# Fewer, longer copies of the sums of v, and a first dense slice converted before the experts begin

## Chip, core and metric

The kernel runs on one core of a Trainium2 chip. The metric is the device time of one execution in microseconds (us), as the median of repeated runs. Engines: PE (TensorE, matmuls and transposes), DVE (VectorE), ACT (ScalarE), POOL (GpSimd), SP (SyncE, which here only sends DMAs).

## What is computed

Three stages on 1536 tokens (2 batches of 768) of width 512 (8 heads of 64):

```python
k_sum = k.reshape(B, H, nb, 32, D).max(axis=3)         # blocks of 32
v_sum = v.reshape(B, H, nb, 32, D).mean(axis=3)
scores = concat([where(|i - j| < 16, q @ k.T / 8, -1e9), q @ k_sum.T / 8 + log(32)])
x = softmax(scores) @ concat([v, v_sum])               # attention, per head
# mixture of experts: tokens with x @ w_skip > 0 go to one of 8 experts (D=512, F=1024)
e = argmax(x @ w_gate); x = x + gate * (relu(x @ w1[e]) @ w2[e])
# dense stage: 512 -> 2048 -> 512
h = x @ w_in; g = where(h >= 1, h, where(h <= -1, 0, (h + 1)**2 / 4)); out = g @ w_out
```

## The kernel before

**Attention** (function `attention`) works on 24 units, twelve per batch. The order of every step is written out by hand as a list of words in `FIRST`; each word is one step, its numbers are its arguments, and each engine executes its own steps in the order of the list. K and k turn q and k (PE transposes, copies by DVE and ACT), S is a unit pair's scores, n and e the maximum and the exponential, T and t turn the probabilities, V multiplies them with v, d, f and x divide. q and lv are loads of q, k and v on SP's queue.

v lies in twelve tiles per batch (`vtile`), three to a buffer of `tails`; rows 0 to 95 of a tile are a window of v, rows 96 to 119 the 24 block sums of v. The sums are made per batch b and half of the heads c: v (three groups of matmuls), u (DVE copies them into `sums`), w (a matmul folds them into PSUM), z (ACT copies the folded sums to `sums`), and then twelve times y (`vgive`, line 361), each copying 24 x 256 sums into one tile. `DIRECT` (line 27) says how many of the twelve are copied directly from PSUM, alternately by ACT and DVE; the others are copied by POOL from `sums`. V of a tile needs its y.

**Routing** is woven into the same list: R, r, L, l compute the gate's scores of one tile of 128 tokens, ga and ia are generators (`r3`, `r4`) of small DVE steps, P is a prefix sum on PE, and sc scatters the finished tiles, by POOL's indirect DMA, into sorted lists in DRAM (`xf`). Tiles go in the groups 0-2, 3-5, 6, 7-8, 9-10, 11. E counts the tokens after tiles 0 to 6; from that ea, ec, ej choose the expert whose tokens form the first block, and `first` gathers it from DRAM. The tokens of a tile stand in one of nine buffers x0 to x8 (`xring`, line 258 for x7 and x8; `XTILE` says which tile uses which); tiles 9 and 10 are in x7 and x8. FX, FA, FB, FD compute the first block (128 tokens of one expert) on PE; FY adds it on DVE and scatters it. lo, ll, lr, le compute the rows of the other blocks; G0 to G3 and GL gather them, once tile 11 has been scattered. lF loads expert weights (1 MB each), W loads a slice of the dense weights (`ff_fetch`).

**Experts and dense stage** (function `experts`) follow the list `ORDER`. Per block p: X, x (transpose and copy), A, a (first matmul, ReLU), T, t, B (second matmul), y (add and scatter); U, P, Q, O are the second part of the largest block. R, r, l transpose the first 512 rows for the dense stage and split them into a high and a low part. Dense slices f = 0 to 15: the weights come as 64-bit numbers, and `bits` (line 1066) makes 32-bit floats of them in three DVE steps (words i, j, k), `high` (H, ACT) and `low` (L, DVE) split them into the two parts in `ffw`. M is the first dense matmul of a slice (12 matmuls of 512 columns), c, S, g, G its activation, N the second (12 matmuls). F fetches expert weights into buffers that earlier blocks free. `st["late"]` names the PSUM buffers in which the blocks' transposes go; M sets it to "h" from the first M on, since N0 takes the "tp" buffers for its results. After the list (`dense.rest`) the remaining slices run in a fixed loop; the dense stage has three chunks of 512 tokens.

Of the kernel before, what the change touches and what calls it, by code (L numbers as in the profile page):

```python
# [43 lines left out]
T7 j8 c5 M6 L7 k8 t7 N3 c6 S5 i9 j9 B7 g5 S6 H8 G5 N4 y7 M7 g6 L8 G6 k9 N5 c7 i10 j10 H9 S7 k10 g7 G7 N6 L9 i11
j11
# [5 lines left out]
K0.2.0 y0.0.1 T1 k0.2.0 q1.0.1 y0.0.0 S4 y0.0.2 z0.0 V0 t1 y0.0.3 y0.0.4 q1.1.1 n4 K0.2.1 e3 y0.0.5 K0.2.2 d0 y0.0.6
k0.2.1 V1 y0.0.7 k0.2.2 K0.2.3 h0.2 y0.0.8 m0.2 T2 y0.0.9 K0.3.0 t2 k0.2.3 y0.0.10 e4 T3 k0.3.0 b0.2 q1.2.0 K0.3.1
y0.0.11 f0 d1 K0.3.2 x0 q1.2.1 k0.3.1 V2 t3 k0.3.2 K0.3.3 h0.3 T4 m0.3 lv1.0.2 v0.1.0 t4 k0.3.3 b0.3 v0.1.1 f1 n5 S6
q1.3.0 x1 e5 d2 V3 f2 n6 v0.1.2 x2 q1.3.1 e6 T5 u0.1 V4 d3 n7 w0.1 K1.0.0 t5 f3 d4 x3 lv1.0.0 S8 y0.1.0 k1.0.0 z0.1
e7 f4 y0.1.2 y0.1.1 V5 x4 y0.1.3 T6 lv1.0.1 n8 y0.1.4 K1.0.1 t6 K1.1.0 d5 y0.1.5 k1.0.1 e8 T7 y0.1.6 k1.1.0 K1.0.2
# [10 lines left out]
S20 ga6 f15 t17 ga6 x15 e19 ga6 d16 P6 f16 E T18 n20 V17 ia6 t18 ea R7 ia6 ea ia6 e20 T19 ec ia6 ea ia6 ec sc6 ea ec
ea x16 r7 S22 ea n21 t19 ea d17 L7 e21 ea f17 ea x17 T20 ea R8 ej ea ej ea V18 ej rege l7 r8 ej n22 V19 t20 d18 n23
e22 T21 lF1.0 f18 lF1.1 d19 first x18 lF1.2 f19 L8 t21 lF1.3 x19 e23 l8 V20 ga7 ga7 R9 ga7 d20 ga7 T22 f20 ga7 x20 p7
V21 r9 ga7 ga7 ga7 P7 t22 d21 L9 f21 ia7 x21 T23 ia7 V22 l9 t23 ia7 R10 ia7 d22 FX ia7 f22 r10 sc7 x22 V23 Fx L10
lF2.0 d23 FA0.0 f23 l10 lF2.1 x23 ga9 R11 ga9 p9 ga9 FA0.1 ga9 r11 ga9 ga9 ga9 L11 ga9 P9 l11 FA0.2 ga11 ia9 ga11 ia9  # L70
# [1299 lines left out]
```

## Time and profile before

| | |
|---|---|
| runs, median (lowest to highest) | 466.08 us (464.23 to 466.92) |
| profiled execution | 467.6 us, span 465.9 us, mean granted clock 0.977 |
| PE busy | 441.9 us (95% of the span) |
| DVE, ACT, POOL busy | 264.8, 208.5, 75.7 us |
| DMA | 73.36 MB, mean 157 GB/s |

How to read it: the page divides the span into 40 slices and gives the busy share of each engine in each; the granted clock is the share of full speed (2.4 GHz) that TensorE got. PE's busy time counts slow matmuls as busy, so a stretch at half clock looks full. The attention takes about the first 93 us, the first block goes to 119 us, experts and dense slices are mixed to about 225 us, and the rest is the dense stage.

### The profile page before, as it was taken

To read this page: it belongs to the slowest core of one execution; us is meant where nothing else is said; L and a number is where in the kernel's file an instruction comes from. 1 tells how busy PE (TensorE), PEld (TensorE's weight loads), DVE (VectorE), ACT (ScalarE), POOL (GpSimd) and SP (SyncE) were. 2 spreads that over 40 slices of the span, in tenths; PEclk is the share of its full clock that TensorE was granted. 3 is DMA by queue.
4 is the path that set the end of the run, shared out by engine and by line. 5 is a ranking of instruction groups with operands and counts; after the bars stand their busy time and mean duration, and the time that the engine had idled before them with its cause. 6 is when DMAs were issued, how large, how long until landed. Compare 5 with 4: busy or idle time off the path is not lost.

```text
span 465.9 us, 8194 instructions
## 1 busy us (share of the span) xinstructions
PE 441.9 (95%) x3100; PEld 319.5 (69%) x3100; DVE 264.8 (57%) x625; ACT 208.5 (45%) x416; POOL 75.7 (16%) x171
## 2 busy tenths in 40 slices
PE   8989999869699999999999999999999999999993
PEld 4657767744345544557888787888888888888872
DVE  5567778925634884888989734333334444334341
ACT  4646668612343233547377764333333343333341
POOL 7314243412610311010100003000000030000003
PEclk9998999979889999999999999999999999999998
DMA  9989729899965999996367001000000020000002
GB/s 181 210 158 217 163 75 380 324 381 393 358 205 214 367 389 389 394 367 203 123 222 271 2 25 69 23 0 1 0 1 1 1 90 1 1 0 1 0 0 97
DMA packets 75008, 73.36 MB, mean 157 GB/s; under 512 B 48926, under 2 KB 57118, under 8 KB 74960
## 3 DMA queue, kind: packets, MB, share of 16 engines
q1 hardware_dynamic: 72144, 64.55, 44.8%
q0 software_dynamic: 2816, 8.20, 4.7%
q8 instruction: 26, 0.43, 0.4%
q14 instruction: 22, 0.18, 0.1%
HBM read 65.66 MB, written 7.70 MB: 157 GB/s over the span
## 4 chain that ended last, share of the span: by engine, by line
issue 50%; PE 17%; DMA 4%; POOL 2%; DVE 1%; SPq 1%; POOLq 0%; ACT 0%; ACTq 0%
PE hf L1134 5%; PE yp L963 4%; PE hp L941 3%; DMA w<-in_moe_w_dram 2%; POOL out_dram L1187 2%; PE yp L1003 1%; DMA x<-xf,re 1%; PE o L1175 1%; PE o L1176 1%; PE o L1177 1%; DVE x L968 1%; PE tph L951 0%; SPq L169 0%; PE tpx L929 0%; POOLq L1166 0%
## 5 line engine op out<-in xcount | busy, mean ns | idle before, releaser
L1134 PE MATMUL hf<-xh,ffw 128*128 128x512 f32 x384 | 127.0, 392 | 0.0
L1134 PEld LDWEIGHTS hf<-xh,ffw 128*128 128x128 f32 x384 | 72.1, 188 | 16.9 <-issue 1.9
L1175 PE MATMUL o<-ffw,g 128*128 128x512 f32 x192 | 76.5, 398 | 0.7 <-ACT g L1158 0.7
L1176 PE MATMUL o<-ffw,g 128*128 128x512 f32 x192 | 75.5, 393 | 0.0
L1177 PE MATMUL o<-ffw,g 128*128 128x512 f32 x192 | 74.9, 390 | 0.0
L1134 PE MATMUL hf<-xl,ffw 128*128 128x512 f32 x192 | 74.9, 390 | 0.0
L1153 DVE TENSOR_TENSOR hf<-hf,c 128x512 f32<-128x512 f32 x48 | 33.5, 698 | 60.0 <-ACT c L1144 43.7
L1143 ACT ACTIVATE hf<-hf,scal 128x512 f32<-128x512 f32 x32 | 21.2, 662 | 85.1 <-DVE c L1142 85.1
L1187 POOL DMA_INDIRECT out_dram<-ob,perm x12 | 11.7, 975 | 223.9 <-DVE ob L1186 160.6
L1162 DVE TENSOR_TENSOR g<-hf,g 128x512 fp32r<-128x512 f32 x48 | 33.1, 690 | 24.9 <-ACT g L1158 24.8
L1142 DVE TENSOR_SCALAR c<-hf 128x512 f32<-128x512 f32 x32 | 22.1, 691 | 37.5 <-PE hf L1134 37.5
L1158 ACT CAST g<-hf 128x512 fp32r<-128x512 f32 x48 | 28.1, 585 | 33.8 <-DVE hf L1153 31.5
L1175 PEld LDWEIGHTS o<-ffw,g 128*128 128x128 f32 x192 | 36.0, 188 | 10.0 <-issue 1.3
L1177 PEld LDWEIGHTS o<-ffw,g 128*128 128x128 f32 x192 | 36.0, 188 | 8.5 <-DVE g L1162 0.4
L1134 PEld LDWEIGHTS hf<-xl,ffw 128*128 128x128 f32 x192 | 36.1, 188 | 8.0 <-DVE xl L1124 0.4
L1176 PEld LDWEIGHTS o<-ffw,g 128*128 128x128 f32 x192 | 36.1, 188 | 6.9
L968 DVE SCALAR_TENSOR_TENSOR x<-yp,x 32x512 f32<-32x512 f32 (+1 forms) x28 | 20.8, 745 | 15.4 <-PE yp L963 14.7
L445 ACT ACTIVATE p<-s,nm 128x120 f32<-128x120 f32 x96 | 26.8, 371 | 5.1 <-DVE nm L439 5.0
L187 POOL DMA_INDIRECT xf<-x,ids x10 | 11.9, 1191 | 81.8 <-DVE ids L213 81.4
L1146 ACT ACTIVATE c<-hf,scal 128x512 f32<-128x512 f32 x16 | 11.0, 689 | 30.7 <-PE hf L1134 30.7
L1144 ACT ACTIVATE c<-c,scal 128x512 f32<-128x512 f32 x32 | 22.8, 712 | 0.0
L941 PE MATMUL hp<-w,xT 128*32 128x256 f32 (+1 forms) x224 | 21.6, 439 | 0.5 <-ACT xT L933 0.5
(224 smaller groups left out, 630.6 us busy)
## 6 DMA issues: line engine op xcount, KB each, us to landing
w<-in_moe_w_dram SPq DMA_DIRECT2D x32, 1024.0 KB, 12.4
raw<-in_moe_w_in_dram SPq DMA_DIRECT2D x16, 512.0 KB, 5.2
raw<-in_moe_w_out_dram SPq DMA_DIRECT2D x16, 512.0 KB, 6.0
pb<-in_v_dram SPq DMA_DIRECT2D x40, 96.0 KB, 3.6
raw<-in_k_dram SPq DMA_DIRECT2D x16, 192.0 KB, 4.4
raw<-in_q_dram SPq DMA_DIRECT2D x16, 192.0 KB, 4.4
x<-xf SPq DMA_DIRECT2D x8, 264.0 KB, 5.5
rows<-xf SPq DMA_DIRECT2D x1, 1024.0 KB
```

What stands on the lines that cost most here:

```text
L445: nc.scalar.activation(out=p[:, u], in_=s[:, u], func=AF.Exp, bias=nm[:, u:u + 1], scale=1.0)
L941: nc.tensor.matmul(hp[a], xT[:, kk], wx[p, 0][:, kk, m * f:m * f + m], start=kk == 0, stop=kk == 3)
L968: nc.vector.scalar_tensor_tensor(out=xg[0:n, 0:512], in0=yp[a], scalar=xg[0:n, 512:513], in1=xg[0:n, 0:512], op0=ALU.mult, op1=ALU.add)
L1134: nc.tensor.matmul(hp, w[:, 128 * kk:128 * kk + 128], a[:, kk], start=(n == 0), stop=(n == 11))
L1142: nc.vector.tensor_scalar(out=c, in0=hp, scalar1=-1.0, scalar2=1.0, op0=ALU.max, op1=ALU.min)
L1144: nc.scalar.activation(out=c, in_=c, func=AF.Square, bias=half, scale=0.5)
L1153: nc.vector.tensor_tensor(out=hp, in0=hp, in1=c, op=ALU.add)
L1158: nc.scalar.copy(out=g[:, 0], in_=hp)
L1162: nc.vector.tensor_tensor(out=o, in0=hp, in1=h.bitcast(F32), op=ALU.subtract)
L1175: nc.tensor.matmul(ops[ch][t], gh[:, a], hi, start=(f == 0), stop=False)
L1176: nc.tensor.matmul(ops[ch][t], gh[:, a], lo, start=False, stop=False)
L1177: nc.tensor.matmul(ops[ch][t], gl[:, a], hi, start=False, stop=(f == NF - 1))
```

## The change

The y words now copy three tiles at once (48 become 16), with the sums repeated by a broadcast; `GIVERS` names the engine of each. The buffers x7 and x8 become one tile, `x78`, whose first 1024 columns hold the bits of dense slice 0. The words i0, j0, k0, W1, H0, L0 go from the beginning of `ORDER` to the end of `FIRST`, as ci, cj, ck, W1, cH, cL. The switch of `st["late"]` goes from M to N. z1.1 is no longer there, as no copy of that half is made by POOL. Both lists are new for all engines: in `ORDER` M0 stands ahead of X0, and A1 ahead of A0.

```diff
-DIRECT = (4, 2), (2, 4)
+GIVERS = (("APPD", "PDPP"), ("ADPP", "ADAD"))
-        xring.extend(per.tile([128, XW], F32, name=f"x{i}") for i in (7, 8))
+        two_x = per.tile([128, 2, XW], F32, name="x78")
+        xring.extend(two_x[:, i] for i in range(2))
+        st["cv0"] = two_x.rearrange("p n c -> p (n c)")[:, 0:1024].rearrange("p (n c) -> p n c", n=2).bitcast(I32)
-        def vgive(b, c, j):
-            to = vtile(b, j)[96:120, 4 * c:4 * c + 4, 0:64]
-            if j >= DIRECT[b][c]:
-                nc.gpsimd.tensor_copy(out=to, in_=sums[c][96:120].rearrange("p (h d) -> p h d", h=4))
-            else:
-                (nc.vector.tensor_copy if j % 2 else nc.scalar.copy)(out=to, in_=st["vo", b, c][96:120])
+        def vgive(b, c, m):
+            to = tails[4 * b + m][96:120, :, 4 * c:4 * c + 4, 0:64]
+            by = GIVERS[b][c][m]
+            x = sums[c][96:120].rearrange("p (h d) -> p h d", h=4) if by == "P" else st["vo", b, c][96:120]
+            {"P": nc.gpsimd.tensor_copy, "D": nc.vector.tensor_copy, "A": nc.scalar.copy}[by](
+                out=to, in_=x.unsqueeze(1).to_broadcast([24, 3, 4, 64]))
 FIRST, before:
-V16 ga6 ia3 ga6 sc3 d15 p6 S20 ga6 f15 t17 ga6 x15 e19 ga6 d16 P6 f16 E T18 n20 V17 ia6 t18 ea R7 ia6 ...
-d22 FX ia7 f22 r10 sc7 x22 V23 Fx L10 lF2.0 d23 FA0.0 f23 l10 lF2.1 x23 ga9 R11 ga9 p9 ...
-FD0.0 Fb1 FD0.1 FD0.2 FD0.3 FD1.0 G0 FD1.1 FD1.2 G1 FD1.3 G2 FY G3 GL
 FIRST, after:
+V16 r7 ga6 S20 ia3 ga6 sc3 t17 d16 ga6 f16 ga6 p6 x16 T18 e19 ga6 n20 L7 V17 ga6 l7 ga6 n21 P6 t18 E e20 ia6 ...
+d22 ia7 FX ia7 f22 ia7 R10 x22 sc7 Fx l9 V23 r10 FA0.0 lF2.0 d23 f23 x23 lF2.1 L10 FA0.1 l10 ga9 ga9 R11 ...
+FD0.0 Fb1 lr ia11 lr sc11 lr lr FD0.1 FD0.2 FD0.3 ci FD1.0 cj FD1.1 ck FD1.2 W1 cH FD1.3 G0 cL G1 FY G2 G3 GL
 ORDER, before:
-Z0 R0 R1 r0 i0 R2 r1 l0 r2 l1 R3 l2 r3 X0 j0 x0 A0 l3 k0 W1 H0 L0 X1 F32 a0 F33 x1 T0 M0 t0 B0 i1 c0 j1 k1 H1 S0
-A1 y0 g0 X2 a1 G0 x2 L1 T1 A2 t1 M1 F50 a2 F40 F41 W2 F51 W4 X3 c1 B1 T2 y1 N0 ...
 ORDER, after:
+Z0 R0 R1 r0 R2 r1 r2 l0 l1 R3 l2 r3 l3 M0 X0 c0 X1 i1 j1 x1 x0 A1 S0 k1 g0 A0 F40 a1 G0 H1 L1 T1 F32 a0 X2 F33
+t1 T0 x2 B1 t0 B0 y1 M1 y0 E6 A2 c1 N0 F50 W2 F41 a2 S1 W3 F51 F42 X3 ...
         def M(f):
-            st["late"] = "h"
             bag["M", f] = dense.mm1(0, f)
+        def N(f):
+            st["late"] = "h"
+            dense.mm2(0, f)
```

## Rows read from the trace of the kernel before

**Rows 1.** PE's timeline: start us, us, engine, line, operation [idle before, releaser].

```profile
33.72 0.62 PE L348 MATMUL vs<-pb,picks 96*32 96x256 f32 x2 [1.26 <-DMA pb<-in_v_dram]
...
90.68 0.64 PE L504 MATMUL lp<-wg,xs 128*64 128x9 f32 x16
...
92.45 0.66 PE L493 MATMUL tpx<-ident,x 128*128 128x128 f32 x4
97.25 1.09 PE L225 MATMUL tpx<-ident,x 128*128 128x128 f32 x4 [4.14 <-DMA x<-xf,r]
```

**Rows 2.** POOL's timeline, same columns, 77 to 108 us.

```profile
77.77 4.21 POOL L364 COPY pb<-sums 24x256 f32<-24x256 f32 x12 [8.20 <-DMA xf<-x,si]
82.25 0.98 POOL L187 DMA_INDIRECT xf<-x,si  x1 [0.28 <-POOL pb L364]
...
86.10 0.98 POOL L187 DMA_INDIRECT xf<-x,si  x1 [0.30 <-DVE be L707]
90.19 1.06 POOL L182 DMA_INDIRECT x<-xf,r  x1 [3.12 <-DVE ohb L546]
...
107.98 0.98 POOL L187 DMA_INDIRECT xf<-x,si  x1 [0.30 <-DVE cnt L646]
```

**Rows 3.** DVE's timeline: tiles 3 to 5, tile 6, and FY.

```profile
76.91 0.29 DVE L596 CAST x<-meta 128x2 int32<-128x2 f32 x3
...
82.05 0.15 DVE L596 CAST x<-meta 128x2 int32<-128x2 f32 x1
...
118.62 0.75 DVE L822 SCALAR_TENSOR_TENSOR x<-yp,x 128x512 f32<-128x512 f32 x1 [6.25 <-PE yp L818]
```

**Rows 4.** The instructions of line 585: duration ns min/median/max, first and last start.

```profile
L585 DVE SCALAR_TENSOR_TENSOR sf<-meta,comp x6: 150/152/422, 64.0 to 109.6; 128x3 f32<-128x3 f32 x2, 128x1 f32<-128x1 f32 x2, 128x2 f32<-128x2 f32 x2
```

**Rows 5.** PE's timeline, 119 to 182 us: R0-R2, A0, A1, B4, A6.

```profile
119.43 1.53 PE L225 MATMUL tps<-ident,rows 128*128 128x128 f32 x12 [0.85 <-DVE x L822]
...
125.23 6.30 PE L941 MATMUL hp<-w,xT 128*64 128x512 f32 x16 [0.51 <-ACT xT L933]
...
139.16 1.93 PE L941 MATMUL hp<-w,xT 128*32 128x256 f32 x32
...
175.28 1.91 PE L963 MATMUL yp<-w,hT 128*32 128x512 f32 x12 [0.51 <-DMA w<-in_moe_w_dram]
...
178.72 3.65 PE L941 MATMUL hp<-w,xT 128*64 128x512 f32 x16
```

**Rows 6.** Windows: length, busy us (x) by engine, granted clock, DMA share, GB/s.

```profile
35.00:40.00 5.00, 5.00 (x75) 3.33 (x74) 3.21 (x10) 2.30 (x7) 1.79 (x5) 0.66 1.20 230
...
125.00:130.00 5.00, 4.77 (x12) 1.49 (x14) 2.77 (x4) 1.22 (x2) 3.09 (x3) 0.50 0.68 256
```

**Rows 7.** The chain that ended last, in order of time: start us, us, what.

```profile
111.23 0.97 DMA xf<-x,si
...
117.99 5.94 DMA x<-xf,re
...
132.88 2.77 PE hf L1134 x12
```

**Rows 8.** Groups by shape: line engine op, out<-in, xcount | busy us, mean ns.

```profile
L1077 DVE SCALAR_TENSOR_TENSOR cv<-raw,cv 128x1024 int32<-128x1024 int32 x16 | 19.6, 1223 | 0.5
...
L1091 ACT CAST ffw<-cv 128x1024 fp32r<-128x1024 f32 x16 | 16.6, 1039 | 7.2 <-DVE cv L1080 7.2
...
L364 POOL COPY pb<-sums 24x256 f32<-24x256 f32 x36 | 12.8, 399 | 30.9 <-ACT sums L359 22.5 <-DMA xf<-x,si 8.2
...
L1074 DVE TENSOR_SCALAR cv<-raw 128x1024 int32<-128x1024 int32 x16 | 11.0, 688 | 5.1 <-DMA raw<-in_moe_w_out_dram 5.0
...
L366 DVE COPY pb<-vso 24x256 f32<-24x256 f32 x6 | 2.6, 430 | 1.9 <-ACT sums L359 1.5 <-PE vso L356 0.2 <-ACT pb L366 0.2
...
L366 ACT COPY pb<-vso 24x256 f32<-24x256 f32 x6 | 2.1, 366 | 3.3 <-PE vso L356 2.8 <-DVE pb L366 0.5
```

More of the change, by code (lines that the diff above doesn't have):

```diff
@@ L44 @@
[L44 to L45 removed]
+Z0 R0 R1 r0 R2 r1 r2 l0 l1 R3 l2 r3 l3 M0 X0 c0 X1 i1 j1 x1 x0 A1 S0 k1 g0 A0 F40 a1 G0 H1 L1 T1 F32 a0 X2 F33
+t1 T0 x2 B1 t0 B0 y1 M1 y0 E6 A2 c1 N0 F50 W2 F41 a2 S1 W3 F51 F42 X3 g1 x3 G1 A3 T2 F60 a3 X4 t2 T3 x4 B2 t3 i2
+j2 N1 y2 A4 k2 B3 a4 W4 H2 E7 F43 F61 L2 F52 U0 F53 T4 u0 y3 X5 t4 P0 x5 i3 A5 j3 p0 k3 P1 a5 W6 H3 F62 L3 T5 i4
+p1 B4 t5 j4 k4 Q0 X6 q0 W5 y4 Q1 F63 x6 H4 F70 A6 q1 L4 M2 a6 i6 O0 c2 j6 k6 W7 H6 S2 g2 L6 G2 T6 i5 X7 o0 M3 x7
@@ L51 @@
[L51 to L55, printed above, removed]
@@ L66 @@
[L66 to L70, printed above, removed]
@@ L71 @@
-p11 ga11 FA0.3 ia9 ga11 ia9 ga11 ia9 FA1.0 Fa0 ga11 rows sc9 ga11 N P11 lF2.2 FA1.1 lo ia11 lF2.3 lo le lo lF3.0 le
-FA1.2 lo le lo le lF3.1 lo ia11 lo FA1.3 ia11 ll lr ll lr ll lr regl ia11 FB0 Fa1 lr ia11 lr sc11 lr FB1 Fb0 lr lr
-FD0.0 Fb1 FD0.1 FD0.2 FD0.3 FD1.0 G0 FD1.1 FD1.2 G1 FD1.3 G2 FY G3 GL
+q0.0.0 q0.0.1 q0.1.0 q0.1.1 Z7 K0.0.0 K0.0.1 lv0.0.0 k0.0.0 k0.0.1 h0.0 m0.0 Z3 K0.0.2 K0.0.3 k0.0.2 lv0.0.1 b0.0
+k0.0.3 Z3 K0.1.0 K0.1.1 k0.1.0 lv0.0.2 k0.1.1 h0.1 m0.1 Z3 K0.1.2 K0.1.3 k0.1.2 b0.1 q0.3.0 k0.1.3 S0 q0.2.0 v0.0.0
@@ new lines @@
+n0 n1 e0 q0.2.1 Z3 v0.0.1 S2 e1 q0.3.1 v0.0.2 lv0.1.1 n2 T0 u0.0 t0 n3 w0.0 e2 K0.3.0 lv0.1.0 T1 k0.3.0 y0.0.0 S4
+z0.0 misc V0 t1 y0.0.3 y0.0.1 e3 T2 d0 n4 y0.0.2 K0.2.0 K0.2.1 f0 lv0.1.2 k0.2.0 V1 t2 k0.2.1 K0.2.2 e4 x0 K0.2.3
+k0.2.2 T3 q1.0.0 k0.2.3 V2 h0.2 m0.2 K0.3.1 t3 K0.3.2 q1.0.1 k0.3.1 T4 b0.2 k0.3.2 K0.3.3 h0.3 q1.2.0 m0.3 v0.1.0 t4
+v0.1.1 k0.3.3 b0.3 q1.1.0 d1 S6 n5 f1 e5 d2 q1.1.1 x1 f2 V3 n6 q1.2.1 T5 x2 e6 d3 V4 n7 v0.1.2 lv1.0.2 f3 d4 t5 x3 S8
+u0.1 e7 f4 x4 w0.1 n8 T6 q1.3.0 z0.1 V5 n9 t6 y0.1.0 K1.0.0 y0.1.1 e8 q1.3.1 T7 y0.1.2 V6 k1.0.0 K1.0.1 lv1.0.0 d5 t7
@@ new lines @@
+L3 ia0 t12 ta ia0 w1.0 ta ia0 e14 v1.1.0 ta ia0 T13 ta ia0 ta sc0 v1.1.1 n15 y1.0.0 S16 ta l3 ta ta z1.0 regt v1.1.2
+t13 y1.0.1 lF0.0 V12 e15 lF0.1 u1.1 R4 d12 lF0.2 n16 w1.1 lF0.3 T14 r4 f12 y1.1.1 W0 y1.1.0 R5 x12 L4 y1.1.2 n17 V13
+r5 y1.1.3 t14 l4 d13 y1.0.2 L5 e16 f13 x13 T15 l5 V14 y1.0.3 ga3 ga3 p3 ga3 S18 t15 ga3 d14 ga3 f14 ga3 e17 x14 T16
+ga3 ga3 n18 R6 V15 ga3 t16 n19 P3 r6 d15 T17 f15 ia3 e18 x15 L6 ia3 R7 ia3 l6 V16 ia3 r7 ga6 S20 ia3 ga6 sc3 t17 d16
+ga6 f16 ga6 p6 x16 T18 e19 ga6 n20 L7 V17 ga6 l7 ga6 n21 P6 t18 E e20 ia6 T19 ea ia6 V18 ea ia6 ec ia6 ea ia6 t19 S22
@@ new lines @@
+ec sc6 ea ec ea d17 e21 ea f17 ea x17 T20 ea d18 R8 ea n22 t20 V19 ea ej r8 T21 ea ej ea ej rege f18 e22 ej x18 n23
+L8 first l8 lF1.0 t21 d19 ga7 f19 lF1.1 ga7 e23 T22 x19 lF1.2 ga7 V20 ga7 lF1.3 ga7 R9 ga7 ga7 p7 d20 ga7 V21 t22 f20
+x20 P7 r9 T23 d21 ia7 f21 V22 ia7 t23 x21 ia7 L9 d22 ia7 FX f22 ia7 R10 x22 sc7 Fx l9 V23 r10 FA0.0 lF2.0 d23 f23 x23
+lF2.1 L10 FA0.1 l10 ga9 ga9 R11 p9 ga9 ga9 ga9 FA0.2 ga9 r11 ga9 ga9 P9 FA0.3 ia9 ia9 ia9 L11 Fa0 ia9 FA1.0 ia9 l11
+rows sc9 ga11 ga11 p11 ga11 FA1.1 ga11 ga11 ga11 ga11 N FA1.2 lo lo le lF2.2 P11 lo le FA1.3 lo le lo lF2.3 le lo
@@ L74 @@
+ia11 lF3.0 lo FB0 Fa1 ia11 ll lF3.1 lr ll lr FB1 Fb0 ll lr ia11 regl lr ia11 FD0.0 Fb1 lr ia11 lr sc11 lr lr FD0.1
+FD0.2 FD0.3 ci FD1.0 cj FD1.1 ck FD1.2 W1 cH FD1.3 G0 cL G1 FY G2 G3 GL
 '''
@@ L859, in attention @@
             P=lambda t: r4p(of[t]), p=lambda t: r4e(of[t]), sc=lambda t: r5(of[t]), C=count_p, E=lambda: count_p(6, 7),
-            N=lambda: count_p(NT, SURE), FX=fb_x, Fx=fb_xc, FA=fb_a, Fa=fb_h, FB=fb_t, Fb=fb_tc, FD=fb_b, FY=fb_y, Z=busy)
+            N=lambda: count_p(NT, SURE), FX=fb_x, Fx=fb_xc, FA=fb_a, Fa=fb_h, FB=fb_t, Fb=fb_tc, FD=fb_b, FY=fb_y, Z=busy, ci=lambda: bits(0, (0,)), cj=lambda: bits(0, (1,)),
+            ck=lambda: bits(0, (2,)), cH=lambda: high(0), cL=lambda: low(0))
         zb = rt.tile([128, 960], BF16, tag="xs", name="zb", bufs=1)[:, 0:480]
@@ L1046, in experts @@
         do = dict(X=X, x=x, A=A, a=a, T=T, t=t, B=B, y=y, U=U, u=u, P=P, p=p_, Q=Q, q=q_, O=O, o=o, Z=Z, R=R, r=r, l=l,
-                  M=M, c=c, S=S, g=g, G=G, N=lambda f: dense.mm2(0, f), H=high, L=low, W=ff_fetch, E=get,
+                  M=M, c=c, S=S, g=g, G=G, N=N, H=high, L=low, W=ff_fetch, E=get,
                   i=lambda f: bits(f, (0,)), j=lambda f: bits(f, (1,)), k=lambda f: bits(f, (2,)),
@@ L1070, in bits @@
                 odd = f % 2 and f > 6
-                cv[f] = st["wk"].tile([128, 2, 512], I32, tag="h" if odd else "cv", name="cv", bufs=2 if odd else 1)
+                if f == 0:
+                    cv[f] = st["cv0"]
+                else:
+                    cv[f] = st["wk"].tile([128, 2, 512], I32, tag="h" if odd else "cv", name="cv", bufs=2 if odd else 1)
             t, o = raw64[f], cv[f]
@@ L1084, in bits, with ff_tile @@
                     ff_fetch(f + 2)
+    def ff_tile(g):
+        if g not in ffw:
+            ffw[g] = wp.tile([128, 2, 4, 512], F32R, tag="w" + FFSLOTS[g], name="ffw")
+        return ffw[g]
     def high(f):
         g = f // 2
-        if f % 2 == 0:
-            ffw[g] = wp.tile([128, 2, 4, 512], F32R, tag="w" + FFSLOTS[g], name="ffw")
+        ff_tile(g)
         nc.scalar.copy(out=ffw[g][:, f % 2, 0:4:2], in_=cv[f].bitcast(F32))
```

24 lines of the change are left out of this document (7 added, 17 removed).

## Prediction

> **What bounds the kernel now.** I read the page's slices first, then the chain that ended last, then the timelines of PE, POOL and DVE between 30 and 180 us, and the windows for the granted clock. PE is busy nearly everywhere, and from the dense slices to the end it has almost no idle time: the last weights that it waits for cost it half a microsecond at 175.28 [rows 5]. So the end of the program moves with the moment from which PE is continuously fed, and that lies around 119 to 141 us. What stands ahead of it is less work than a row of round trips through DRAM. PE stands still for 4.14 us ahead of 97.25, until the gather of the first block has landed [rows 1]. That gather was issued at 90.19, because the scatter of tile 6 was issued only at 86.10, because the scatters of tiles 3 to 5 were issued only from 82.25, behind twelve copies of the sums of v on POOL, 4.21 us from 77.77 [rows 2]; their data had been ready since 77.2, the end of the cast at 76.91, and those of tile 6 since 82.2 [rows 3]. The second round trip is the scatter of tile 11, issued at 111.23: when it has landed, the gathers of the other blocks go, at 117.99, and the first of them takes 5.94 us [rows 7]. PE meanwhile ends the first block at 118.6, waits 0.85 us for the DVE operation that empties its result, does the transposes of the R words, waits again, and starts block 0 (word A0) at 125.23 [rows 3, 5]. The third loss is the clock: in 125 to 130 us the granted clock is 0.50, that is 1.2 GHz, after this thin stretch [rows 6]; A0 takes 6.30 us where the same shape later takes 3.65 [rows 5], so 2.65 us are lost there.
>
> **The change, part by part.** *Sums of v.* Out go 36 copies on POOL at 0.399 us, 6 on DVE at 0.430, 6 on ACT at 0.366 [rows 8] and one copy of the sums by ACT (z1.1). In come 7 on POOL, 5 on DVE and 4 on ACT, each of three times the elements. No row shows such a copy; it is bounded below by one old copy and above by three (1.20, 1.29 and 1.10 us). I take three throughout, since nothing excludes it: POOL 14.4 to 8.4 us, DVE 2.6 to 6.5, ACT 2.2 to 4.4. What DVE and ACT get in work lies in the attention, beside PE, which sets the pace there; I cost it at nothing, and at up to 1 us if a copy stands ahead of a softmax step that PE waits for. On the path only one place counts: behind the scatters of tiles 0 to 2 there are now two long copies instead of twelve short ones, 2.4 us instead of 4.2 (bounds 0.8 and 2.4).
>
> One operation of DVE with two inputs in SBUF (L585) runs six times: 0.152 us in the median, 0.422 at the longest [rows 4], and that one lies amid the twelve copies. The Trainium skill has the rule for it, and it speaks against long copies (SBUF — State Buffer, the part on the ports): VectorE and GpSimd share a pair of ports, held for a whole instruction, so such a DVE operation waits out a GpSimd copy. The trace agrees. By the rule a DVE operation may now wait up to 1.2 us once instead of 0.27 several times; but two copies hold DVE for at most their own 2.4 us, against 4.2 before, so the sum would not grow.
>
> *The order of the attention.* PE waited 1.26 us at 33.72 for the last load of v of its batch [rows 1], and its clock was at half for a part of 35 to 40 us [rows 6]. T5 and V4 now stand ahead of that step. The later loads come at their own pace, so little of this can last; I take 0.4 us, bounds 0 and 0.9.
>
> *The first gather.* With two copies the scatters of tiles 3 to 5 start at 77.77 + 2.4 + 0.3 = 80.5 and, at their spacing of 1.28 us (82.25 to 86.10 is three of them [rows 2]), that of tile 6 can go at 84.3. The new list puts P6 and E, on which tile 6 and the choice of the first block rest, behind R7, L7, T18 and V17; four steps of these kinds take 2.4 us (from 90.68 to 93.11, four lines of which [rows 1] has the first and last). So tile 6's data come at 82.2 + 2.4 - 0.4 = 84.2, just in time. The gather then goes 4.1 us after tile 6's scatter, as it did, at 88.4: **1.8 us gained**. Bounds: 3.0, if PE is earlier still, and nothing, if the choice of the block, which the same 2.4 us delay, comes last. PE is there before that in either kernel. R10 (0.66 us [rows 1]) moved behind this wait and P9 ahead of L11; counted word by word, the PE work from here to P11, and so to tile 11's scatter, is the same in both lists.
>
> *First dense slice.* ci, cj, ck, cL are 0.69 and three times 1.22, 4.35 us of DVE, and cH 1.04 us of ACT [rows 8] (cL is taken as the others of its shape), moved from among the R words to the end of the first block. DVE is idle there for 6.25 us [rows 3], so the work itself is covered. But the bits now stand in the buffers of x7 and x8, which hold tiles 9 and 10: ci must wait until their scatters (the second issued at 107.98 [rows 2]) have been read out. Tile 11's scatter freed its gather after 6.8 us (111.23 to 117.99 [rows 7]); with the same time tiles 9 and 10 are free at 114.7, and the five steps one after another end at 120.1. FY, which empties the first block, stands behind cL in the list, and R0 on PE waits for FY. It ran at 118.62 [rows 3] and would run at 120.1: **1.5 us lost**; bounds 0 (the scatter lands so much sooner) and 5 (below). Queued behind ci on DVE are only cj, ck, cL, FY and the put of the first block, for which nobody waits soon.
>
> *W1.* Its two loads (1 MB) are now ahead of the gathers on SP, which has nothing else to send then. If they slow the gather of block 0, M0 covers it: the gather lands near 122 and X0 now stands behind M0, which ends past 125. The bits of slice 1 no longer wait for its load.
>
> *M0 before X0.* One slice is 12 matmuls, 2.77 us [rows 7]; it now runs while PE would wait for the gather and for x0. The later switch of "late" lets the blocks use other PSUM buffers until N0, which first needs them: nothing.
>
> **The sum.** Before: R0 starts at 119.43, and at 139.16 + 1.93 = 141.1 the words R, X0, A0, X1, T0, M0, B0 and A1 are done [rows 5]. After: R0 at 119.43 - 1.8 + 1.5 = 119.1; R is 1.53 for three words [rows 5], 0.66 for the fourth (four transposes, [rows 1]) and 0.6 for the wait between them, an estimate; 0.8 for the copy and subtraction of the last quarter, also one; M0 from 122.7 to 125.5; X0 and X1 0.8, the copy of x 0.4, A1 1.93, A0 3.65, T0 0.66, and B0, as many matmuls of A0's width, 3.65: 136.6. That is **4.5 us gained at 2.4 GHz**. But a thin stretch is still there: 2 us with PE idle ahead of R0, then transposes. The clock fell after both thin stretches in [rows 6], so I expect it to fall again, now under M0. In 35 to 40 us a mean of 0.66 makes 3.4 us at half clock, which cost half of that, 1.7; at A0 it cost 2.65. I take 1.7, since M0 follows R with hardly a gap. Net **2.8 us**. The profiled execution took 467.6 us with a span of 465.9; it lies 1.5 us above the median of the runs, 466.08. Against the profiled one the forecast is 464.8, against the median 463.3.
>
> **The rivals.** *The clock does not fall.* M0 fills the stretch well enough and all 4.5 us stay: 461.6. For it: M0 begins some 2.5 us sooner than A0 did. Against it: R0 is hardly earlier than before. *The gain is given back on the way.* At 175.28 PE reached B4 just as its weights came [rows 5]; if the loads do not move up with PE, it waits there and the end stays: 465.5. Against it: A1 now stands ahead of A0 and frees its buffer sooner, so loads start sooner, and slice 1 is loaded earlier. *Slower: DVE is stuck behind the scatters of tiles 9 and 10.* It is the 1.5 us above, grown. If those tiles are free not 6.8 but 12 us after the issue, FY and R0 come 5.2 us later still and the longer fall of the clock (0.9 more) follows: 463.3 + 6.1 = 469.4. The gain is used up when they come 2.8 us late. For it: the scatters share the DMA engines with the weights then. Against it: tile 11's took 6.8 in the same traffic. A new stall of PE in the attention would cost microsecond for microsecond in the same way.
>
> **How the numbers follow.** The forecast has 0.40 and 463.3, no fall of the clock 0.22 (461.6), given back 0.18 (465.5), slower 0.20 (469.4). 0.5% (2.3 us) is about what a measurement of this kernel can tell from no change, so the bounds are 463.7 and 468.4: of the forecast 0.26 lies below and 0.14 between, the second case wholly below but for 0.01, a part of the slow one between. Faster 0.47, same 0.34, slower 0.19. The range, 459.8 to 468.0, takes in the unknown costs (3.0 instead of 1.8 at the gather; 2.65 instead of 1.7 at the clock) and the beginning of the slow case.
>
> **What would show it.** In the new trace: the scatters of tiles 3 to 5 behind two POOL copies, and the first gather near 88.4; ci about 6.8 us after the scatter of tile 10; FY behind cL; R0 near 119; M0 directly behind R, and A0 at 3.65 us or little more. I am wrong if the first gather is not earlier, if FY runs past 121, or if PE waits for weights between 140 and 180.

## The result, and the profile after

The changed kernel takes 471.73 us in the median (469.90 to 472.98), the kernel before 465.15 in the same series: a ratio of 1.0119, with a 95% interval of 1.0069 to 1.0168. It is slower; 463.3 was forecast, and the range ended at 468.0. Timed again on two chips (d and e below) the ratio was 1.0175 (1.0116 to 1.0234) and 1.0049 (1.0019 to 1.0080). Ratios leave out executions more than 1.5% above the fastest of their kernel, and they differ by up to 0.4% from the quotient of the two medians (1.0141 here), so a few tenths of a per cent say little. The profiled execution took 471.34 us, 3.7 more than the one of before, where the medians are 6.6 apart: the profiled execution of before (467.6) is a long one, and the two traces show only a part of the loss.

| | before | after |
|---|---|---|
| span, mean granted clock | 465.9 us, 0.977 | 469.6 us, 0.981 |
| PE, DVE, ACT, POOL busy | 441.9, 264.8, 208.5, 75.7 us | 442.8, 266.1, 208.5, 68.1 us |
| first gather issued | 90.19 | 89.65 |
| R0 starts | 119.43 | 117.32 |
| B4 ends | 177.19 | 180.59 |

No engine does more work worth speaking of. Up to R0 the changed kernel is 2.1 us ahead; by B4 it is 3.4 us behind, and from there the two run alike.

The lead up to R0 is not the forecast's. The first gather is only 0.5 us earlier, but PE, itself later, waits 0.38 us for it where [rows 1] has 4.14, and the granted clock stays at 1.00 from 95 to 105 us, where the kernel before has 0.65 and 0.67. PE's wait after, then the windows from 95 us on, before and after:

```profile
95.58 0.66 PE L222 MATMUL tpx<-ident,x 128*128 128x128 f32 x4 [0.38 <-DMA x<-xf,r]
```

```profile
95.00:100.00 5.00, 2.75 (x36) 2.45 (x36) 0.34 (x2) 0.59 (x1) 0.38 (x1) 0.65 1.00 354
95.00:100.00 5.00, 4.62 (x53) 2.99 (x51) 2.23 (x16) 1.29 (x3) 1.99 (x2) 1.00 1.05 350
```

PE's timeline of the changed kernel, which answers [rows 5] (start us, us, engine, line, operation, idle time before and its releaser):

```profile
117.32 3.53 PE L222 MATMUL tps<-ident,rows 128*128 128x128 f32 x16 [2.24 <-DVE x L821]
...
125.02 0.83 PE L929 MATMUL tpx<-ident,x 64*128 64x64 f32 x8
128.08 6.83 PE L941 MATMUL hp<-w,xT 128*32 128x256 f32 x48 [2.24 <-ACT c L1157]
135.57 0.44 PE L951 MATMUL tph<-ident,h 128*128 128x128 f32 x2 [0.66 <-ACT h L945]
...
137.37 0.91 PE L951 MATMUL tph<-ident,h 128*128 128x128 f32 x4 [0.99 <-ACT h L945]
138.21 6.89 PE L963 MATMUL yp<-w,hT 128*32 128x512 f32 x32
...
148.01 1.93 PE L941 MATMUL hp<-w,xT 128*32 128x256 f32 x32
...
178.68 1.91 PE L963 MATMUL yp<-w,hT 128*32 128x512 f32 x12 [1.36 <-DMA w<-in_moe_w_dram]
```

R, then M0 from 121.53, then X0 and X1 follow as forecast. Then three things stand there that the forecast had not: 2.24 us ahead of A1 and A0 (one group of 48), 1.65 us in two waits ahead of T1 and T0, and 1.36 us at B4, where [rows 5] has 0.51. A1 with A0, and B1 with B0, also ran partly at half clock (0.50 in 128 to 130 and in 138 to 140 us): they took 6.83 and 6.89 us, where the traces below have 5.52 and 5.51 at 2.4 GHz. The windows of the granted clock, which answer [rows 6] (length, busy us by engine, clock, DMA share, GB/s):

```profile
115.00:120.00 5.00, 2.76 (x14) 2.54 (x14) 2.76 (x5) 1.46 (x3) 3.73 (x4) 0.72 1.06 377
120.00:125.00 5.00, 4.10 (x17) 2.77 (x16) 2.02 (x3) 1.17 (x2) 1.97 (x3) 0.94 1.04 384
125.00:130.00 5.00, 2.76 (x29) 1.64 (x32) 0.00 (x0) 3.02 (x6) 1.95 (x2) 0.74 1.04 363
```

What held PE stands on ACT and DVE. ACT first, then DVE, same columns as for PE:

```profile
125.25 0.69 ACT L1155 ACTIVATE c<-hf,scal 128x512 f32<-128x512 f32 x1 [3.78 <-DMA x<-xf,re]
...
127.16 0.72 ACT L1158 ACTIVATE c<-c,scal 128x512 f32<-128x512 f32 x1
127.79 0.52 ACT L933 COPY xT<-tpx 128x128 f32<-128x128 f32 x2
134.65 0.59 ACT L1167 CAST g<-hf 128x512 fp32r<-128x512 f32 x1 [6.34 <-DVE hf L1162]
135.13 0.39 ACT L945 ACTIVATE h<-hp 128x256 f32<-128x256 f32 x1
...
136.73 0.59 ACT L945 ACTIVATE h<-hp 128x512 f32<-128x512 f32 x1
```

```profile
110.95 0.69 DVE L1080 TENSOR_SCALAR x<-raw 128x1024 int32<-128x1024 int32 x1 [1.97 <-DMA xf<-x,si]
...
116.53 0.74 DVE L821 SCALAR_TENSOR_TENSOR x<-yp,x 128x512 f32<-128x512 f32 x1
...
132.05 0.69 DVE L1080 TENSOR_SCALAR cv<-raw 128x1024 int32<-128x1024 int32 x1 [9.86 <-DMA raw<-in_moe_w_out_dram]
132.78 1.23 DVE L1083 SCALAR_TENSOR_TENSOR cv<-raw,cv 128x1024 int32<-128x1024 int32 x1
133.92 0.69 DVE L1162 TENSOR_TENSOR hf<-hf,c 128x512 f32<-128x512 f32 x1
```

On ACT the four operations of c0 (125.25 to 127.9) stand ahead of the copies x1 and x0, which A1 and A0 need. On DVE i1 waits until 132.05 for the load of W1, 9.86 us; behind it in the list stand j1 and S0; g0 on ACT waits for S0 (6.34 us), and behind g0 stand a1 and a0, the ReLUs that T1 and T0 need. The third wait is read from the chain that ended last (start us, us, what):

```profile
118.38 13.55 DMA raw<-in_moe_w_out_dram
132.05 0.70 DVE cv L1080
...
148.08 1.91 PE hp L941 x32
150.01 0.37 SPq L166
150.42 0.47 SPq L1064
150.94 7.66 DMA raw<-in_moe_w_out_dram
158.69 0.70 DVE cv L1080
...
163.70 1.14 DVE cv L1086
...
166.97 11.67 DMA w<-in_moe_w_dram
178.68 1.91 PE yp L963 x12
```

A2 ends at 149.9; only then can SP send F50, and W2, queued behind F50, goes at 150.42 (145.69 in the kernel before). When W2 has landed i2 runs; k2 frees a buffer, W4 and F43 follow, and F43 holds the weights that B4 waits for. The new list has A2 behind B1, B0 and M1.

The copies of the sums, grouped by shape (duration in ns, least, median and most), and POOL's timeline, which answer [rows 8] and [rows 2]:

```profile
L364 POOL COPY pb<-sums x7: 826/832/835, 20.9 to 72.1; 24x768 f32<-24x768 f32 x7
L364 DVE COPY pb<-vso x5: 964/965/967, 20.9 to 69.0; 24x768 f32<-24x768 f32 x5
L364 ACT COPY pb<-vso x4: 789/795/799, 19.8 to 68.2; 24x768 f32<-24x768 f32 x4
```

```profile
71.29 1.60 POOL L364 COPY pb<-sums 24x768 f32<-24x768 f32 x2 [6.92 <-DMA xf<-x,si]
78.00 0.98 POOL L184 DMA_INDIRECT xf<-x,si  x1 [5.11 <-DVE mn L539]
...
84.74 0.98 POOL L184 DMA_INDIRECT xf<-x,si  x1 [3.20 <-DVE n L697]
89.65 1.06 POOL L179 DMA_INDIRECT x<-xf,r  x1 [3.93 <-DVE x L481]
```

POOL's two copies are done at 72.9, 9 us sooner than the twelve of [rows 2]. It then waits for DVE, and the first gather is 0.5 us earlier, not 1.8.

### The profile page after: what moved, and what is told of

The parts are those of the page before. It is cut to its first block, busy times and chain, and to the rows that moved or that the text cites. A ratio compares the mean times of both kernels' runs of the same rounds, so it can differ in the third digit from the quotient of the medians.

```text
span 469.6 us, 8155 instructions
## 1 busy us (share of the span) xinstructions
PE 442.8 (94%) x3100; PEld 319.5 (68%) x3100; DVE 266.1 (57%) x624; ACT 208.5 (44%) x413; POOL 68.1 (15%) x142
## 4 chain that ended last, share of the span: by engine, by line
issue 50%; PE 29%; DMA 9%; SPq 5%; DVE 3%; POOL 2%; ACT 1%; POOLq 0%; DVEq 0%
DMA raw<-in_moe_w_out_dram 5%; PE hf L1143 4%; PE yp L963 3%; PE xo L468 3%; DMA w<-in_moe_w_dram 2%; PE pt L450 2%; SPq L166 2%; PE tpk L373 2%; PE s L432 2%; POOL out_dram L1196 2%; PE hp L941 2%; PE yp L1003 1%; PE vs L347 1%; PE hp L800 1%; DMA x<-xf,r 1%
## 5 line engine op out<-in xcount | busy, mean ns | idle before, releaser
L1167 ACT CAST g<-hf 128x512 fp32r<-128x512 f32 x48 | 28.1, 585 | 37.5 <-DVE hf L1162 37.4
L184 POOL DMA_INDIRECT xf<-x,ids x10 | 13.1, 1309 | 85.9 <-DVE ids L210 85.6
L963 PE MATMUL yp<-w,hT 128*32 128x512 f32 (+1 forms) x128 | 21.2, 646 | 1.8 <-DMA w<-in_moe_w_dram 1.4
```

Source lines behind the costliest of these rows:

```text
L963: nc.tensor.matmul(yp[a], hT[:, c, a], wx[p, 1][:, m * f + c], start=c == 0, stop=c == m - 1)
L1167: nc.scalar.copy(out=g[:, 0], in_=hp)
```

## The experiments

Three theories, each the rival of the others: the hold of S0 by i1, which waits for W1's load (theory 1); c0 ahead of x1 and x0 (theory 2); the chain from A2 over F50 and W2 to B4 (theory 3). A fourth place is the attention, if its new list costs by itself. The series ran on four chips, called b to e here; of the result above (a) the chip is not recorded. Ratios are to the kernel before on the same chip, and only ratios of one chip are compared directly.

**Which half loses.** The old attention with the new expert part (and the early conversion), and the new attention with the old expert part, the latter on two chips.

```diff
 first kernel: FIRST and vgive of before, then
+... FD0.3 ci FD1.0 cj FD1.1 ck FD1.2 W1 cH FD1.3 G0 cL G1 FY G2 G3 GL     and ORDER of after
 second kernel: FIRST and GIVERS of after, but
+... FD0.3 FD1.0 G0 FD1.1 FD1.2 G1 FD1.3 G2 FY G3 GL                       and ORDER of before
```

> The attention, its list and its copies of the sums of v as in the kernel before; the early conversion of slice 0 (ci to cL, W1), M0 ahead of X0 and the new expert list as in the changed kernel. If the loss lies in the expert part: 465.2 + 4 to 6, 469 to 471, with the same pair of PE waits near 128 and 136. If the late choice of the first block in the new attention list (fetches 2.6 us later, hence W1 later) is what makes it lose, the weights start at 87.6 again, W1 lands 2.6 us sooner, i1 waits until about 129.5, and the time is 465.2 to 467.

> The attention, its new list and the long copies of the sums of v as in the changed kernel, up to the first block; the early conversion is left out of that list, and the expert part and its list are those of the kernel before. The prediction's step (two long copies let the scatters of tiles 3 to 5 and then the first gather go 1.8 us sooner, and the time follows): 464.5 at 466.3 for the kernel before, ratio 0.996. Rival A, from the traces so far (tile 6's scatter at 84.7 to 87.3 instead of 86.1, first gather at 89.7 to 93.1 instead of 90.2, and the expert weights start 2.6 us later): nothing gained in the first block, ratio 1.000 to 1.003. Rival B, the new attention alone costs what the changed kernel lost: ratio 1.010.

> New attention, long copies, old expert list, as before in a run on another chip (0.9995). If the new attention is what suffers from the idle time without a releaser, the ratio is 1.004 or more on a chip that has it; if both attentions suffer alike, 0.998 to 1.001 on any chip. The prediction's step would give 0.996.

Experts alone: 1.0094 (1.0061 to 1.0128, chip b). Attention alone: 0.9995 (0.9965 to 1.0024, chip c) and 0.9941 (0.9911 to 0.9970, chip e). So the expert part loses by itself on b, and the attention does not on c and e. The attention alone was never run on a, b or d, where PE has the idle time told of in the last section; what it costs there is not shown.

**The two waits.** One list edit each: slice 1's conversion behind a0; x1 and x0 ahead of c0; both; both with the old attention.

```diff
-M0 X0 c0 X1 i1 j1 x1 x0 A1 S0 k1 g0 A0 F40 a1 G0 H1 L1 T1 F32 a0 X2 F33 t1 T0 x2 B1 t0 B0
+M0 X0 c0 X1 x1 x0 A1 S0 g0 A0 F40 a1 G0 T1 F32 a0 i1 j1 k1 X2 F33 t1 T0 x2 B1 t0 H1 L1 B0     (i1 behind)
+M0 X0 X1 i1 j1 x1 x0 c0 A1 S0 ...                                                             (c0 behind)
```

> Only the expert list is edited: i1, j1, k1, H1, L1 (bits and conversion of slice 1, which wait for the load of W1) go behind S0, g0, G0 and a0. Theory 1 (the wait for W1's load on DVE holds S0, behind it g0 on ACT, behind that a1 and a0): DVE's 9.86 us wait at 132.05 no longer stands ahead of S0; S0 runs right behind c0, near 128.5; PE's two waits ahead of T1 and T0 (0.66 and 0.99 us) go, A2, F50, W2 and B4 come 1.7 us sooner: 1.7 us less than the changed kernel's 471.7, so 470.0. Theory 2 (c0 on ACT ahead of x1 and x0 costs 2.24 us and the clock, and this alone counts): within 0.5 us of 471.7, since c0 stays where it is. Rival, the late load itself: slice 1's conversion, now last, makes M1 wait, and the time is 471.7 or more.

> Only the expert list is edited: x1 and x0 stand ahead of c0 on ACT. Theory 2: PE's wait of 2.24 us at 128.08 shrinks to about 0.5, A1 and A0 take some 5.6 us instead of 6.83 as the clock falls less, and all later work comes 2 to 3 us sooner: 469 to 469.7. Theory 1: A1 and A0 come sooner, but a1 and a0 still stand behind g0, which waits for S0, which waits for i1 and j1 until 133.9; PE then waits at T1 for what it saved at A1, T1 stays at 135.5 and the time at 471.7 within 0.5.

> Both edits of the two kernels before. If theory 1 is right (the two waits lie one behind the other, and the second hides the first), the gain is more than the sum of the single ones: T1 at 131.5 to 132.5, A2 near 144.5 instead of 148.0, W2 issued near 147 and B4 near 175.5; 467.5 to 468.5, hence still 2 to 3 us slower than the kernel before. If the loss of the changed kernel against the kernel before lies in these two places alone, it comes to 465 or below. If it lies in the weights that are fetched later (the fetches of 90 to 116 us start 2.6 us later), PE waits for weights at B4 whatever the two waits do, and the time stays over 470.

> Attention, its list and its copies as in the kernel before; early conversion, M0 ahead of X0, and the expert list with both edits (i1 to L1 behind a0, x1 and x0 ahead of c0). The two edits were worth 1.2% with the new attention. If that is a matter of the expert list alone, the same edits take the ratio of experts alone from 1.009 to 0.998 here. If the new attention is what makes the repaired list lose its gain again, this one is well below 0.998; if the new attention had brought something, it stays above 1.002.

On chip b: i1 behind 1.0063 (1.0023 to 1.0103), c0 behind 1.0122 (1.0073 to 1.0170), both 1.0003 (0.9967 to 1.0040). Both with the old attention, on chip c: 1.0037 (1.0005 to 1.0068). With i1 behind, moving c0 as well brings 0.6%; with c0 behind, moving i1 as well brings 1.2%. Both together did better than expected (1.005 to 1.007). The changed kernel itself was not run on b; against its 1.0119 of the first series, moving c0 alone brings nothing. PE's timeline with c0 behind shows why:

```profile
128.12 5.52 PE L941 MATMUL hp<-w,xT 128*32 128x256 f32 x48 [0.47 <-ACT xT L933]
139.39 0.69 PE L951 MATMUL tph<-ident,h 128*128 128x128 f32 x2 [5.75 <-ACT h L945]
```

The wait ahead of A1 is gone (0.47) and A1 and A0 run at full clock, but PE then stands 5.75 us ahead of T1: a1 is behind g0, S0 and i1, and in that execution W1 landed at 135.7.

**W1 earlier instead of i1 later.** The cause taken away at its other end: `W1` in `FIRST` ahead of lF2.2, that is ahead of the last four expert fetches of that list (the expectation says six).

> The changed kernel with one edit in the first list: W1 goes ahead of the last six expert fetches on SP. Theory 1: W1 lands by about 112, DVE does i1 and j1 right behind the R words near 122, S0 no longer waits for a load, PE's waits ahead of T1 and T0 go as with i1 moved behind: ratio 1.006 instead of 1.012. Rival: the expert weights behind W1 come 2.7 us later and PE waits for them in A1, A0 or B1: ratio 1.012 or more.

1.0014 (0.9984 to 1.0044, chip c). SP sent W1 at 99.73, i1 ran at 120.49, and PE waited neither at T1 nor at T0; the 2.24 us behind c0 were still there. This is no test of theory 1, though: on chip c PE did not wait at T1 with the late W1 either (in W2 early alone, below, i1 ran 10.0 us after R0, and R0 to A2 took 29.3 us, as here), and the changed kernel itself was not run on c. What shows theory 1 is the pair on b, c0 behind and both.

**The chain to B4.** Both edits, and W2 sent behind F40 instead of behind F50, k2 ahead of y2; the same with W1 early too; this third edit alone on the changed kernel; and its like on the kernel before.

```diff
-A0 F40 a1 ... A2 c1 N0 F50 W2 F41 ... t3 i2 j2 N1 y2 A4 k2 B3
+A0 F40 W2 a1 ... A2 c1 N0 F50 F41 ... t3 i2 j2 k2 N1 y2 A4 B3
 on the kernel before:
-F33 x1 T0 ... F41 W2 F51 ... E6 y2 A3 N1 a3 i2 j2 E7 X4 T3 k2
+F33 W2 x1 T0 ... F41 F51 ... E6 i2 j2 k2 y2 A3 N1 a3 E7 X4 T3
```

> Both edits, and in addition W2 stands ahead of F50 on SP (behind F40) and k2 ahead of y2 on DVE. Theory 3 (the chain A2, F50, W2, its landing, i2, y2, k2, W4, F43 sets when B4's weights come, and the new list has A2 behind B1, B0 and M1): W2 is issued near 133 instead of 150, W4 near 156 instead of 164, F43 lands before 172, PE doesn't wait at B4 (1.4 to 1.5 us there with both edits), and the ratio goes from 1.000 to 0.997 or below. Rival: B4's weights are late by the mere bytes queued ahead of them, or PE then waits at another fetch: ratio 1.000, with a wait of 1 us or more somewhere between 150 and 230.

> The kernel with both edits and W2 early (ratio 0.994), and in addition W1 ahead of the last six expert fetches. Theory 1 says that the early W1 (1.012 to 1.001 alone) and i1 moved behind a0 remove the same wait, so together they bring nothing more: 0.993 to 0.996. If the early load had a gain of its own (less traffic while the gathers and A1 run), the ratio is 0.990 or below; if the six fetches behind it come too late, 0.997 or above.

> The changed kernel with only the third edit: W2 behind F40 instead of behind F50, k2 ahead of y2. Theory 3 as a cause of its own: PE's 1.36 us at B4 go and with them 0.3 to 0.6% (ratio 1.006 to 1.009), since the chain to B4 no longer runs over A2. If the wait at B4 is only where an earlier loss shows, taking it away brings nothing: 1.010 to 1.014.

> The kernel before with the third edit alone: W2 behind F33 instead of behind F50 and F41, i2, j2, k2 ahead of y2. There PE waits 0.51 us at B4. If the gain of the third edit is one that any version would have had, the ratio is 0.994 to 0.997 here too; if it belongs to the new list, which reaches B4 sooner, the most is the 0.51 us: ratio 0.998 to 1.001.

All three edits 0.9941 (0.9889 to 0.9992): faster than both kernels. With W1 early as well 0.9946 (0.9914 to 0.9977): nothing more, as theory 1 says. The third edit alone 1.0007 (0.9970 to 1.0043); its expectation started from the 1.012 of the first series, and without the changed kernel on c its gain there is not known (on e the changed kernel is at 1.0049). On the kernel before 1.0002 (0.9969 to 1.0035), no gain that the times show, though its stretch from A2 to B4, in the table below, is shorter too (26.6 us; 27.9 to 28.3 with the old list otherwise). All four on chip c. With W2 early PE no longer waits at B4:

```profile
168.73 2.08 PE L963 MATMUL yp<-w,hT 128*32 128x512 f32 x16
```

**Three losses or one.** The missing pairs with the changed kernel itself (chip d), then the changed kernel and all three edits with the new and the old attention (chip e).

> The changed kernel with i1 to L1 behind a0 and W2 early; c0 stays ahead of x1 and x0. From the traces so far, R0 to the end of A2 takes 28 us with i1 moved and 25.4 to 26.9 with c0 moved too; the end of A2 to the end of B4 takes 27.8 to 27.9 with W2 early, 30.5 to 31.0 without. If the three are separate losses: 0.55% over the kernel with all three edits (0.994), so 0.999 to 1.000, with PE's wait of 2.2 us ahead of A1 still there. If c0's place costs nothing by itself: 0.994.

> The changed kernel with x1 and x0 ahead of c0 and W2 early; i1 and j1 stay ahead of S0. If the hold of S0 by i1 hides what c0's new place saves (theory 1), the time is that of W2 early alone, 1.001, and PE waits ahead of T1 instead of A1. If c0 counts by itself, 0.995.

> The changed kernel as it is. By the segments (2.6 us from A2 to B4, nothing else) it lies 0.56% above W2 early alone, at 1.006 to 1.007. If it is at 1.010 to 1.013 again, the early W2 brings more than the stretch from A2 to B4.

> The changed kernel as it is, as the base of the other three. 1.012 to 1.018 on a chip with idle time of PE without a releaser between 56 and 90 us; near 1.006 on one without, by the 0.56% that W2's chain costs over the kernel with W2 early (1.001 there).

> All three edits in the expert list (i1 to L1 behind a0, x1 and x0 ahead of c0, W2 and k2 early), new attention. 1.6 to 1.8% less than the changed kernel in this call if the expert list's loss is the same on every chip: 0.994 where the changed kernel is at 1.012, 1.000 where it is at 1.017.

> All three edits, but attention and copies of the kernel before. 0.56% less than both edits with the old attention (1.004): 0.998. If it is below the kernel with the new attention in this call, the new attention costs; if above, it gains.

Chip d: changed 1.0175 (1.0116 to 1.0234), i1 and W2 1.0090 (1.0051 to 1.0129), c0 and W2 1.0081 (1.0048 to 1.0113). Chip e: changed 1.0049 (1.0019 to 1.0080), all three 0.9952 (0.9922 to 0.9982), all three with the old attention 0.9976 (0.9943 to 1.0009). The ratios alone don't add up from chip to chip, so the profiled executions are compared instead, one for each run and up to 5 us from the median of its run. In each the span is cut at the start of R0, the end of A2 (for the old list the end of B1, by which the same words are done, and X3, 0.4 us) and the end of B4, where both lists have done the same matmuls. From B4 to the end all take 288.7 to 289.6 us.

| profiled execution | chip | to R0 | R0 to A2 | A2 to B4 |
|---|---|---|---|---|
| before | | 119.4 | 29.7 | 28.1 |
| attention alone | c, e | 116.9, 119.7 | 29.6, 28.4 | 27.9, 28.3 |
| before, W2 early | c | 117.9 | 29.9 | 26.6 |
| changed | a, d | 117.3, 119.7 | 32.6, 32.7 | 30.7, 30.7 |
| changed | e | 115.3 | 29.4 | 30.5 |
| experts alone | b | 119.2 | 28.7 | 30.5 |
| i1 behind | b | 118.7 | 28.1 | 31.0 |
| c0 behind | b | 119.9 | 34.8 | 30.5 |
| W1 early | c | 115.6 | 29.3 | 30.5 |
| both edits, new and old attention | b, c | 124.0, 122.8 | 25.4, 26.0 | 30.5, 30.6 |
| W2 early alone | c | 118.6 | 29.3 | 27.9 |
| i1 and W2 | d | 117.6 | 28.6 | 28.1 |
| c0 and W2 | d | 123.8 | 27.1 | 28.3 |
| all three, and with W1 | c | 116.1, 119.6 | 26.9, 25.4 | 27.8, 27.8 |
| all three, new and old attention | e | 120.7, 122.1 | 27.1, 26.9 | 27.7, 27.8 |

Read by columns, there are three losses. From A2 to B4 the new list takes 30.5 to 31.0 us unless W2 goes early, and 27.7 to 28.3 then: 2.6 us (0.56%), in every execution. No two runs of the new list on one chip differ in W2 alone, so this rests on the stretches and on PE's wait at B4, 0.7 to 1.5 us without the early W2 and gone with it. From R0 to A2 it takes 28.1 to 29.4 us with c0 ahead, hardly less than the old list, and 25.4 to 27.1 with x1 and x0 ahead: 2 to 3 us. In three executions (changed on a and d, c0 behind) it took 32.6 to 34.8: these are the ones in which PE waited at T1, where W1 landed and i1 began 14.7, 14.9 and 15.9 us after the start of R0. In the others with i1 in its old place it began 4.9 to 13.2 us after it (4.9 with W1 early, 13.2 with the changed kernel on e), and PE did not wait at T1. So the hold by i1 is a matter of when the load lands, c0 costs by itself where the hold doesn't hide it, and W2's chain costs in every trace of the new list.

The three losses do not explain everything. On chip d all three ratios missed their expectations, and in one direction: 1.0175 for 1.006 to 1.007 (or 1.013 at most), 1.0090 for 1.000 at most, 1.0081 for 1.001 at most. Some 0.5 to 1% there has no cause shown. On chip e the three edits brought 1.0% and not 1.6 to 1.8%: the changed kernel's trace there has no wait at T1.

To R0 the times differ by 9 us between executions of like lists, which would be enough to keep the ratios from adding up. What the traces show of it is told in the last section; how much of the excess on chip d it makes up was not measured.

## Why the prediction was wrong

In the table's terms the forecast was: R0 0.3 us sooner, R0 to A2 2.5 us shorter (4.2, less 1.7 for the clock), the rest as before. It came out: 2.1 sooner, 3.0 longer, 2.5 longer. Three steps failed: the copy of x priced at 0.4 us, slice 1's bits taken not to wait for their load, and the loads up to B4 taken to move up with PE. They cost 1.8, 1.65 and 2.5 us in this trace, more than the whole gain of 4.5 that was forecast at full clock.

- **Copies.** Right in kind, sizes near the lower bounds: 0.83, 0.96 and 0.79 us, about twice the old ones of [rows 8], not three times; 1.60 us on the path instead of 2.4. The rule on the shared ports was seen at work, see the last section: it held two operations for 1.2 us in all, within the 2.4 allowed.
- **Attention and first gather.** The wait for v at 33.72, of which 0.4 us was taken as a gain, is gone, and the clock in 35 to 40 us is 1.00, not the 0.66 of [rows 6]. The scatters of tiles 3 to 5 had been held by twelve copies in [rows 2]; now their data are what comes last, in all these traces. On chips c and e the first gather went at 84.6 to 87.5 against 88.4 forecast; in the time this shows on e alone (0.9941, and 0.9995 on c, where 0.996 would have been the forecast). On a, b and d, where PE stood still in the attention, the scatter of tile 6 came at 84.7 to 87.3, not 84.3, and the gather at 89.7 to 93.1. The 4.1 us from that scatter to the gather were too few everywhere: 4.3 to 6.1 in these traces.
- **R0.** It came 1.8 us sooner than forecast by luck. PE was late at the first gather, hardly waited for it, and the clock did not fall there as it had before (the lines are in the section on the result); the forecast had no such term.
- **Slice 0 and FY.** Right. ci ran 6.9 us after the scatter of tile 10 (104.06), FY came behind cL, and PE waited 2.24 us ahead of R0 instead of 0.85: 1.4 us lost, 1.5 forecast. The slow rival (FY 5 us late behind the scatters) did not come.
- **M0 before X0.** M0 came where forecast, 121.53 to 125.1, but from R0 to its end took 7.8 us and not 6.4: R ran partly at half clock (0.50 in 118 to 120 us), and PE stood for 0.91 us in two waits at M0. What failed is the term behind it, "the copy of x 0.4". The 0.4 was taken from the list of PE, with X0 behind M0, and not from that of ACT, where c0 stands between X0 and x0. Four operations, 2.6 us, are there, and PE waits 2.24 us; with the clock that follows, 2 to 3 us.
- **W1.** The step "the bits of slice 1 no longer wait for its load" was the worst one. It looked at when SP is free, and not at what SP had sent: four fetches of 1 MB from 105.94 on, behind which the load took 13.55 us to land. Nor did it ask what is queued behind i1 on DVE: S0, then by way of g0 on ACT the ReLUs a1 and a0, and so T1, T0, B1 and B0. That is 1.65 us of PE in this trace, and 5.75 where c0 did not hide it.
- **The clock.** It fell, as forecast, but under R and behind M0 rather than under M0, and cost more than 1.7: 1.3 us at A1 and A0 and 1.4 at B1 and B0.
- **Given back at B4.** This rival came true beside the others, and was under-priced: at 465.5 it only took the gain away. The argument against it, that A1 ahead of A0 starts the loads sooner, was true of F40 alone. F50 waits for A2, W2 is queued behind F50, and A2 had moved behind B1, B0 and M1. 2.5 us. Of the prediction's signs of being wrong this is the one that came: PE waited for weights between 140 and 180.

Together the two stretches came out 5.5 and 2.5 us worse than forecast, R0 1.8 better, the end 0.3 worse: 6.5, the difference between the forecast for the profiled execution and its time. Between the medians the miss is 8.4 (463.3 and 471.73); the other 1.9 us no trace shows.

## What to carry to other kernels

When a list is made anew, follow each moved word on the queue of every engine that runs a part of it: what it waits for, and what now stands behind it there; on a DMA queue too, where a load can land late behind what was sent before it (13.55 us for W1 here, 7.66 for W2) and cannot be sent before the buffer of its neighbour ahead is free. Cut the span at points where both lists have done the same work and compare the stretches; ratios of single edits may not add up when one wait hides another. A conversion that waits for a load belongs behind the work that others wait for, and a load that starts a chain of buffers belongs ahead of one that waits for a matmul.
